# A down tile, late transposes and the prologue's order in an attention and gated-FFN kernel

## The chip, the core and the metric

The kernel runs on one core of a Trainium2 chip. Its time is device microseconds of one launch, as the median of several. The engines of the core work side by side, each on its own queue in the order in which its instructions were written: PE (TensorE) does matmuls, ACT (ScalarE) activations, DVE (VectorE) element-wise work and reductions, POOL (GpSimd) a few small operations, and SP (SyncE) issues nearly all DMAs. They wait for one another through semaphores.

## The reference

The input x has 2048 rows of 512 numbers in bf16. The output is a pre-norm transformer block:

```
h   = x + softmax(q k^T / 4) v @ wo      # q, k, v = layernorm(x) @ wqkv, 32 heads of 16
out = h + (sigmoid(g) * u) @ w_down      # g, u = layernorm(h) @ w_gate, layernorm(h) @ w_up
```

The inner width of the FFN is 1792, which is 14 blocks of 128.

## The kernel before

The prologue loads x, takes the layer norm of the 16 row tiles in pairs (`stats`, `apply`, `trans`), multiplies the first 128 columns of k for all rows (`k_mm`, four heads to a group of 64 columns) and of q for the first 512 rows, and finds a bound on the scores from the norms of q and k, so that the softmax needs no maximum. `k_copy` takes a product of k to SBUF on ACT and sends it to its place by a DMA on SP.

Then come 683 steps. The queries are cut into five chunks, three of 512 rows and two of 256 (`CHUNKS`); in each, 8 groups of four heads go over all keys. A step (`emit_scores`) multiplies the scores of three units of 128 x 512 into the three banks of one of two tiles `pss` (L879), and takes their exponential on ACT (L890). On every fourth step, and some others, ACT takes two banks and DVE computes the third with integer and polynomial operations spread over four steps: L909, L912 and L915, L918, L922. The products with v (`emit_pv`, L961) follow some steps later, mostly on steps whose number is 2 modulo 4, into the one bank `acc`. At the end of each group `emit_norm` copies `acc` (L935), sends the sums through DRAM with DMAs on SP, takes reciprocals (L946) and scales (L942) at fixed later steps.

PSUM has eight banks: six belong to `pss`, one is `acc`, and the last, `pm` (pool `ps_misc`, one buffer), serves everything else while the steps run. This other work is the generator `filler`: the products of v, k and q for later groups, and the FFN of each chunk after its attention is complete. `emit_fill` takes matmuls from it after each step, by a budget (`rate`, per step modulo 4; zero where the step has three PV groups). The generator yields 1 for a matmul, `("at", n)` to go on at the next step that is n modulo 4, `("gap", n)` to leave steps out, `("from", n)` to wait for step n, and `("rate", n)` to set a budget that holds until it is taken back. Deferred work on DVE is put into `later(step, fn)`, which runs ahead of the fill of that step.

The FFN of a chunk is `ffn_tasks`. `ffn_wo_tight`, used for chunks 2 and 3, multiplies a tile of 128 rows with wo in two halves of four matmuls (L598), adds x on DVE (L607), takes statistics (L145, L146, L150, and POOL's power at L152), applies the norm two steps later (L156), and transposes the normalized tile into `pm` (L162) after the next tile's wo. L163 copies the transposed tile to `hnT` on DVE. `ffn_up` takes the 14 blocks in gate and up products (L622), with the tanh (L627) on ACT and the product of both (L635) on DVE, one block to a `pm` tile in chunk 2 and two (of 256 columns each) in chunk 3. `ffn_down` multiplies each tile with w_down in 14 matmuls (L638), and `down_out` forms the output (L643) and stores it (L645).

For the last chunk `wo_early` puts seven of the wo matmuls of the first tile into the steps; the rest is the tail, `ffn_last`, where no attention runs. Its own norm is a chain over DVE, POOL and ACT. While it runs, `spin` keeps PE busy with matmuls into `acc` whose result nobody reads (L253). Then come the last transposes (L791), the copies of h (L806), gate and up blocks, and the down matmuls (L823).

Of the kernel before, what the change touches and what calls it, by code (L numbers as in the profile page):

```python
# [11 lines left out]
FP32 = mybir.dt.float32  # L12
# [7 lines left out]
def kernel(  # L20
# [199 lines left out]
    def k_spread(ku, g, cols, eng):  # L220
        eng.dma_start(out=KT[0:P:2, g, cols], in_=ku[64 * (g % 2):64 * (g % 2) + 64, cols])
# [42 lines left out]
    def prologue(pro):  # L264
# [103 lines left out]
        def k_chunk(n):  # L368
            ps = k_mm(n)
            square(n, ps[:])  # L370
            k_copy(n, ps)
# [47 lines left out]
        apply(4)  # L419
        trans(4)  # L420
        norm_part_of(0)
        k_chunk(1)
        stats(6)
        apply(5)
        trans(5)
        norm_mm_to(acc[:], sqs["q"])
        v0 = v_prod(0, pm_tile())
        v_cast(0, v0)
# [28 lines left out]
        half_copy(0)  # L457
        half_copy(1)
        k_spread(ku, 0, slice(3 * QC, S), nc.sync)
        pn3 = ps_misc.tile([P, 512], FP32, name="pm")  # L460
        norm_half(pn3, 7)
        k_max(pn3[:, 0:QC // 2], km2[:, 2:3])
        v_cast(1, v_prod(1, ps_misc.tile([P, 512], FP32, name="pm")))
        m2 = k_most()
        sqrt_bits(z0[:], m2[:])
        nc.vector.tensor_scalar(out=bnd[0:32, :], in0=y0[0:32, :].bitcast(FP32), scalar1=z0[0:32, :].bitcast(FP32),
# [196 lines left out]
    def ffn_wo_tight(c):  # L663
        turn = None
        for tt, t in enumerate(tiles_of(c)):
            xr = x_load(t)
            yield ("at", 3)
            ps = pm_tile()
            for g in range(NG):
                if g == NG // 2:  # L670
                    yield ("at", 0)
                yield 1
                wo_mm(ps, c, tt, g)
            hn = wo_ln(ps, xr, tt)
            if turn:
                yield ("at", 1)
                yield 1
                hn_transpose(*turn)
            turn = (tt, hn)
        yield ("gap", 1)  # L680
        yield ("at", 1)
        yield 1
        hn_transpose(*turn)

    def ffn_up(c):
        w = CHUNKS[c][1]
        at = cycle((3, 1) if c + 2 < NC else (3, 0, 1))
        for fs in blocks_of(w):
            yield ("at", next(at))
            psg = pm_tile()  # L690
            for i, f in enumerate(fs):
                for k in range(DC):
                    yield w / QC
                    ffn_mm(wg, psg, w, f, i, k)
            sg = gate_act(psg)
            yield ("at", next(at))
            psu = pm_tile()
            for i, f in enumerate(fs):
                for k in range(DC):
                    yield w / QC  # L700
                    ffn_mm(wu, psu, w, f, i, k)
            up_mul(psu, sg, fs, w)

    def ffn_down(c, tight):
        at = 0
        for tt, t in enumerate(tiles_of(c)):
            for f in range(FC):
                if tight:
                    if f % 3 == 0:
                        yield ("at", (3, 0, 1)[at % 3])  # L710
                        at += 1
                elif f % 5 in (0, 3):
                    yield ("at", 0 if f % 5 else 3)
                if f == 0:
                    psd = pm_tile()
                yield 1
                down_mm(psd, f, tt)
            down_out(psd, t, tt)
# [12 lines left out]
    def wo_early(c):  # L731
        early["x"] = [x_load(t) for t in tiles_of(c)]
        early[0] = pm_tile()
        for g in range(NG - 1):
            if g == NG - 2:
                yield ("from", NS - 4)
            yield 1
            wo_mm(early[0], c, 0, g)

    def ffn_last(c):  # L740
        q0, w = CHUNKS[c]
        ts = tiles_of(c)
        n = len(ts)
        sums, rb = pm_tile(), pm_tile()
        pss = [early[0]] + [pm_tile() for _ in range(n - 1)]
        xrs = early["x"]

        def wo(tt, g0, g1):
            for g in range(g0, g1):
                wo_mm(pss[tt], c, tt, g)  # L750

        def add_x(tt):
            nc.tensor.matmul(pss[tt][:], lhsT=ident_bf[:], rhs=xrs[tt][:], start=False, stop=False)

        xs = norm_part(xs_all, w, NG - 1)
        nc.vector.tensor_copy(out=xs, in_=acc[:, 0:w])
        wo(1, 0, 2)
        for q in range(n):
            nc.tensor.matmul(sums[:, 4 * q:4 * q + 4], lhsT=xs[:, q * P:(q + 1) * P],
                             rhs=ident_f[:, DH:P:32], start=True, stop=True)  # L760
        wo(1, 2, 6)
        r16 = small.tile([P, 4 * n], FP32, name="r16")
        nc.vector.reciprocal(out=r16[:], in_=sums[:, 0:4 * n])
        rx = norm_part(rb_all, w, NG - 1).rearrange("p (t j d) -> p t j d", t=n, j=4)
        wide = r16[:].rearrange("p (t j) -> p t j", j=4).unsqueeze(3).to_broadcast([P, n, 4, 32])
        nc.vector.tensor_copy(out=rx[:, 0], in_=wide[:, 0])
        nc.scalar.copy(out=rx[:, 1], in_=wide[:, 1])
        for tt in range(n):
            nc.tensor.matmul(rb[:, tt * P:(tt + 1) * P], lhsT=rx[:, tt].rearrange("p j d -> p (j d)"),
                             rhs=ident_f[:], start=True, stop=True)  # L770
        nc.vector.tensor_tensor(out=OT[c % 2][:, NG - 1, 0:w], in0=xs, in1=rb[:, 0:w], op=ALU.mult)
        ready.add(("o", c, NG - 1))
        wo(1, 6, NG - 1)
        add_x(0)
        add_x(1)
        for tt in range(n):
            wo(tt, NG - 1, NG)
        spin(acc, wo_pad[:, 0, :], 6)
        mv = small.tile([P, n, nc.vector.BN_AGGR_DIM], FP32, name="mvl")
        nmr = small.tile([P, 1], FP32, name="nmr")  # L780
        rss = []
        hns = [pmh["work"].tile([P, D], BF16, name="xn", tag="xn") for _ in range(n)]

        def stats(tt):
            ln_stats(pss[tt][:], mv[:, tt, :])
            rss.append(ln_rstd(mv[:, tt:tt + 1, :], 1))

        def turn(tt, copy):
            pt = pm_tile()[:].bitcast(BF16)[:, 0:4 * P].rearrange("p (b q) -> p b q", b=4)
            for b in range(4):  # L790
                nc.tensor.transpose(out=pt[:, b, :], in_=hns[tt][:, b * P:(b + 1) * P], identity=ident_bf[:])  # L791
            copy(out=hnT[:, :, tt * P:(tt + 1) * P], in_=pt)

        stats(0)
        ln_stats(pss[1][:], mv[:, 1, :])
        nc.vector.tensor_scalar(out=nmr[:], in0=mv[:, 0, 0:1], scalar1=rss[0][:, 0:1], scalar2=-1.0,
                                op0=ALU.mult, op1=ALU.mult)
        nc.scalar.activation(out=hns[0][:], in_=pss[0][:], func=ACT.Identity, scale=rss[0][:, 0:1], bias=nmr[:])
        rss.append(ln_rstd(mv[:, 1:2, :], 1))
        ln_apply(hns[1][:], pss[1][:], mv[:, 1, :], rss[1][:, 0:1])  # L800
        turn(0, nc.scalar.copy)
        spin(acc, wo_pad[:, 0, :], 2)
        turn(1, nc.vector.tensor_copy)
        spin(acc, wo_pad[:, 0, :], 2)
        for tt in range(n):
            nc.vector.tensor_copy(out=h_sb[:, tt, :], in_=pss[tt][:])  # L806
        for fs in blocks_of(w):
            psg = pm_tile()
            for i, f in enumerate(fs):
                for k in range(DC):  # L810
                    ffn_mm(wg, psg, w, f, i, k)
            sg = gate_act(psg)
            psu = pm_tile()
            for i, f in enumerate(fs):
                for k in range(DC):
                    ffn_mm(wu, psu, w, f, i, k)
            up_mul(psu, sg, fs, w)
        for tt, t in enumerate(ts):
            for cols in ((0, D),) if tt < n - 1 else ((0, D // 2), (D // 2, D)):
                cs = slice(*cols)  # L820
                psd = pm_tile()
                for f in range(FC):
                    nc.tensor.matmul(psd[:, cs], lhsT=hT[:, f, tt * P:(tt + 1) * P], rhs=wd[:, f, cs],  # L823
                                     start=(f == 0), stop=(f == FC - 1))
                ob = pmh["work"].tile([P, D], BF16, name="ob", tag="xn")
                nc.vector.scalar_tensor_tensor(out=ob[:, cs], in0=psd[:, cs], scalar=0.5, in1=h_sb[:, tt, cs],
                                               op0=ALU.mult, op1=ALU.add)
                nc.sync.dma_start(out=out_v[:, t, cs], in_=ob[:, cs])

# [145 lines left out]

    def emit_fill(i):
        state["step"] = i
        r = rate(i)
        if not r or state["done"] or i < state["wait"]:
            state["debt"] = 0.0  # L980
            return
# [128 lines left out]
```

## Time and profile before

| what | us |
|---|---|
| median of three runs | 958.11 (957.77 to 960.41) |
| the profiled execution | 958.45 |
| its span | 956.6 |
| first exponential (step 0) starts | 29.82 |
| step 533, first of the late transposes of chunk 2 | 713.85 |
| step 647, first gate block of chunk 3 | 871.19 |
| step 679 | 921.54 |
| end of the last exponential (step 682) | 926.60 |
| first gate block of the tail | 935.30 |
| the stores at the end are issued by | 954.59 |

The step starts are the starts of the L890 rows of the timeline. A row of the timeline has start, length, engine, line, operation, what it writes and reads, and how many instructions were merged into it; in brackets stands how long the engine was idle before it and which instruction ended the wait. A group of rows can merge several steps. The granted clock of TensorE was 1.00 throughout (0.99 in the last 20 us).

### The profile page before, as it was taken

The numbers are of one execution on the slowest core, as the hardware profiler recorded it, in microseconds if no ns is written. First come the engines' busy times: TensorE is split into PE (matmuls) and PEld (weight loads), VectorE is DVE, ScalarE is ACT, GpSimd is POOL, SyncE is SP. The second block draws the span as 40 slices with busy tenths as digits, with TensorE's granted clock in tenths as the row PEclk, the third lists the DMA queues.
The fourth block names the chain that finished last, engine by engine and source line by source line (L and its number), as shares of the span: only waits on it lengthen the run. The fifth ranks groups of instructions, "written<-read, shape, count | busy, mean of one in ns | idle before, by whom it ended". The sixth has DMA issues, their size and how long they took to land.

```text
span 956.6 us, 17273 instructions
## 1 busy us (share of the span) xinstructions
PE 839.0 (88%) x6433; PEld 336.9 (35%) x6433; DVE 783.3 (82%) x1413; ACT 898.2 (94%) x778; POOL 40.0 (4%) x56
## 2 busy tenths in 40 slices
PE   5998888888788999998788999988788999998998
PEld 3322222222222322222222323222355555455656
DVE  7589988888788888899888888898898788777653
ACT  6889999999999999999999999999998999999872
POOL 5600000000000000000000000000000000000000
PEclk9999999999999999999999999999999999999999
DMA  5102350000003000000010000000010000110010
GB/s 161 24 2 56 115 117 16 16 16 14 16 14 103 15 16 17 20 24 23 4 26 27 16 17 16 19 9 27 16 31 23 17 10 15 27 32 16 10 35 12
DMA packets 37645, 28.45 MB, mean 30 GB/s; under 512 B 17788, under 2 KB 32920, under 8 KB 37560
## 3 DMA queue, kind: packets, MB, share of 16 engines
q1 hardware_dynamic: 37416, 27.22, 10.8%
q8 instruction: 50, 0.82, 0.4%
q14 instruction: 35, 0.29, 0.1%
q10 hardware_dynamic: 144, 0.13, 0.0%
HBM read 20.31 MB, written 2.61 MB: 24 GB/s over the span
## 4 chain that ended last, share of the span: by engine, by line
PE 45%; ACT 24%; DVE 22%; issue 6%; DMA 2%; SPq 1%; POOL 0%; ACTq 0%; DVEq 0%
PE pss L879 21%; ACT pt L890 13%; PE acc L961 8%; PE pm L622 7%; ACT stg L890 4%; ACT wd L890 4%; DVE stg L909 2%; PE pm L638 2%; ACT QTu L890 2%; PE pm L598 2%; PE pm L171 2%; DVE y L918 2%; DVE pt L922 2%; DVE reg L912 1%; DVE reg L635 1%
## 5 line engine op out<-in xcount | busy, mean ns | idle before, releaser
L879 PE MATMUL pss<-QB,KT 128*128 128x512 bf16 (+3 forms) x2554 | 476.0, 337 | 80.7 <-ACT pt L890 40.2
L890 ACT ACTIVATE pt<-pss 128x1536 bf16<-128x1536 f32 (+1 forms) x392 | 502.2, 1366 | 14.0 <-PE pss L879 9.5
L879 PEld LDWEIGHTS <-KT 64*128 64x128 bf16 (+1 forms) x2554 | 179.3, 95 | 340.5 <-issue 232.8
L890 ACT ACTIVATE stg<-pss 128x1536 bf16<-128x1536 f32 (+1 forms) x140 | 183.4, 1361 | 5.0 <-PE pss L879 3.8
L909 DVE TENSOR_SCALAR stg<-pss 128x512 int32<-128x512 f32 x123 | 84.8, 690 | 68.1 <-PE pss L879 59.9
L961 PE MATMUL acc<-pt,Vaug 128*17 128x512 bf16 (+1 forms) x1471 | 112.5, 338 | 2.3 <-DVE pt L922 1.1
L890 ACT ACTIVATE wd<-pss 128x1536 bf16<-128x1536 f32 (+1 forms) x80 | 103.9, 1391 | 1.9 <-PE pss L879 1.4
L890 ACT ACTIVATE QTu<-pss 128x1024 bf16<-128x1024 f32 (+1 forms) x71 | 95.9, 1350 | 1.7 <-PE pss L879 1.3
L915 DVE SCALAR_TENSOR_TENSOR y<-reg 128x512 f32<-128x512 f32 x123 | 85.2, 692 | 4.2
L918 DVE SCALAR_TENSOR_TENSOR y<-y,reg 128x512 f32<-128x512 f32 x123 | 84.3, 685 | 1.1
L961 PEld LDWEIGHTS <-Vaug 128*17 128x17 bf16 x2560 | 49.2, 89 | 94.7 <-issue 80.3
L622 PE MATMUL pm<-reg,reg 128*128 128x512 bf16 (+1 forms) x280 | 57.9, 337 | 7.9 <-DVE reg L635 7.6
L622 PE MATMUL pm<-reg,wu 128*128 128x512 bf16 (+1 forms) x280 | 58.1, 338 | 1.4 <-ACT sg L627 1.1
L638 PE MATMUL pm<-wd,reg 128*128 128x512 bf16 x196 | 55.6, 382 | 1.9 <-DVE ob L643 1.9
L912 DVE TENSOR_SCALAR reg<-stg 128x512 int32<-128x512 int32 x123 | 52.0, 422 | 1.8
L961 PE MATMUL acc<-stg,Vaug 128*17 128x256 bf16 (+1 forms) x564 | 50.6, 326 | 0.3 <-DVE stg L922 0.2
L635 DVE SCALAR_TENSOR_TENSOR reg<-sg,pm 128x512 bf16<-128x512 f32 x56 | 38.2, 683 | 14.2 <-PE pm L622 13.8
L922 DVE SCALAR_TENSOR_TENSOR pt<-y,stg 128x512 bf16<-128x512 f32 x70 | 48.0, 686 | 2.0
L152 POOL TENSOR_TENSOR rs<-ve,pw_neg 128x1 f32<-128x1 f32 x16 | 11.8, 735 | 877.1 <-DVE ve L150 870.5
L627 ACT ACTIVATE sg<-pm 128x512 f32<-128x512 f32 x56 | 36.5, 651 | 10.4 <-PE pm L622 9.9
L909 DVE TENSOR_SCALAR wd<-pss 128x512 int32<-128x512 f32 x45 | 31.0, 689 | 17.9 <-PE pss L879 16.5
L171 PE MATMUL pm<-reg 128*128 128x512 bf16 x124 | 38.3, 398 | 1.8 <-DVE stg L526 0.7
(151 smaller groups left out, 715.8 us busy)
## 6 DMA issues: line engine op xcount, KB each, us to landing
rb_all<-rd SPq DMA_DIRECT2D x96, 64.0 KB
xr<-in_A_x_dram SPq DMA_DIRECT2D x16, 128.0 KB
out_dram<-ob SPq DMA_DIRECT2D x15, 128.0 KB
rb_all<-rd SPq DMA_DIRECT2D x60, 32.0 KB
reg<-in_A_x_dram SPq DMA_DIRECT2D x7, 256.0 KB
KT<-stg SPq DMA_DIRECT2D x7, 256.0 KB
reg<-in_B_w_gate_dram SPq DMA_DIRECT2D x4, 448.0 KB
wu<-in_B_w_up_dram SPq DMA_DIRECT2D x4, 448.0 KB
```

Of the source, the lines that this page charges most:

```text
L171: nc.tensor.matmul(ps[:], lhsT=wqkv_sb[:, c, w0:w0 + P], rhs=xnT[:, c, n * QC:(n + 1) * QC], start=(c == 0), stop=(c == DC - 1))
L622: nc.tensor.matmul(ps[:, i * w:(i + 1) * w], lhsT=wt[:, c, f * P:(f + 1) * P], rhs=hnT[:, c, 0:w], start=(c == 0), stop=(c == DC - 1))
L635: nc.vector.scalar_tensor_tensor(out=out, in0=a, scalar=1.0, in1=b, op0=ALU.add, op1=ALU.mult)
L638: nc.tensor.matmul(ps[:], lhsT=hT[:, f, tt * P:(tt + 1) * P], rhs=wd[:, f, :], start=(f == 0), stop=(f == FC - 1))
L879: nc.tensor.matmul(pss[:, ui, h * w:(h + 1) * w], lhsT=KT[rows, g, kt * P:(kt + 1) * P], rhs=QB[n_qg % 2][rows, j, 0:w], start=True, stop= ...
L890: ex = nc.scalar.activation(out=pt[:, 0:na, :], in_=pss[:, 0:na, :], func=ACT.Exp, scale=DH ** -0.5 / QS)
L909: return nc.vector.tensor_scalar(out=e_bits, in0=src, scalar1=ONE_BITS, scalar2=0.0, op0=ALU.add, op1=ALU.max)
L912: nc.vector.tensor_scalar(out=e_man, in0=e_bits, scalar1=0x7FFFFF, scalar2=-0x40800000, op0=ALU.bitwise_and, op1=ALU.bitwise_or)
L915: nc.vector.scalar_tensor_tensor(out=e_pol, in0=m, scalar=PA, in1=m, op0=ALU.add, op1=ALU.mult)
L918: nc.vector.scalar_tensor_tensor(out=e_pol, in0=e_pol, scalar=PB, in1=e_man.bitcast(FP32), op0=ALU.add, op1=ALU.mult)
L922: nc.vector.scalar_tensor_tensor(out=dst, in0=e_pol, scalar=PC, in1=e_bits.bitcast(FP32), op0=ALU.add, op1=ALU.mult)
L961: nc.tensor.matmul(acc[32 * j:32 * j + VW, 0:w], lhsT=Vaug[:, kt, 4 * g + j, :], rhs=p[:, h * w:(h + 1) * w], start=(kt == 0), stop=(kt == ...
```

## The change

There are four parts.

In the prologue, the ACT copy of the second 512 columns of k (`k_copy(1)`) goes behind the copy of the transposed tiles 10 and 11 (`trans(5)`). The product of v for tile 1 goes into `acc` instead of `pm`, with two of its four matmuls ahead of the last norm product (`norm_half(pn3, 7)`) and two behind it.

The transposes in `ffn_wo_tight` ask for a step that is 2 modulo 4 instead of 1. These are four tiles in chunk 2 (steps 533, 537, 541, 545 become 534, 538, 542, 546) and two in chunk 3 (641, 645 become 642, 646). `emit_fill` lets fill run on such a step while a rate is set.

The gate and up blocks of chunk 3 are put on five steps out of eight instead of six out of eight.

The down matmuls of the last tile of chunk 3 leave the steps. They stand in the tail in the place of the six `spin` matmuls ahead of the norm's transposes; their output is formed after the copies of h, which now take two other rows of `h_sb`. The early wo matmuls of the last chunk follow directly, and the seventh of them comes after the last PV.

```diff
@@ prologue
-        k_chunk(1)
+        ps1 = k_mm(1)
+        square(1, ps1[:])
         stats(6)
         apply(5)
         trans(5)
+        k_copy(1, ps1)
...
+        for c in range(2):
+            v_mm(acc, 1, c)
         pn3 = ps_misc.tile([P, 512], FP32, name="pm")
         norm_half(pn3, 7)
         k_max(pn3[:, 0:QC // 2], km2[:, 2:3])
-        v_cast(1, v_prod(1, ps_misc.tile([P, 512], FP32, name="pm")))
+        for c in range(2, DC):
+            v_mm(acc, 1, c)
+        v_cast(1, acc)
@@ ffn_wo_tight, twice
-                yield ("at", 1)
+                yield ("at", 2)
                 yield 1
                 hn_transpose(*turn)
@@ ffn_up
-        at = cycle((3, 1) if c + 2 < NC else (3, 0, 1))
+        at = cycle((3, 1) if c + 2 < NC else (3, 1, 3, 0, 1))
@@ ffn_down
-        for tt, t in enumerate(tiles_of(c)):
+        for tt, t in enumerate(tiles_of(c)[:None if c < NC - 2 else -1]):
@@ wo_early
-                yield ("from", NS - 4)
+                for _ in range(3):
+                    yield ("from", NS + LAG)
@@ ffn_last
-        spin(acc, wo_pad[:, 0, :], 6)
+        psd = pm_tile()
+        for f in range(FC):
+            down_mm(psd, f, len(tiles_of(c - 1)) - 1)
...
         for tt in range(n):
-            nc.vector.tensor_copy(out=h_sb[:, tt, :], in_=pss[tt][:])
+            nc.vector.tensor_copy(out=h_sb[:, n + tt, :], in_=pss[tt][:])
+        down_out(psd, tiles_of(c - 1)[-1], len(tiles_of(c - 1)) - 1)
...
-                nc.vector.scalar_tensor_tensor(out=ob[:, cs], in0=psd[:, cs], scalar=0.5, in1=h_sb[:, tt, cs],
+                nc.vector.scalar_tensor_tensor(out=ob[:, cs], in0=psd[:, cs], scalar=0.5, in1=h_sb[:, n + tt, cs],
@@ emit_fill
-        r = rate(i)
+        r = rate(i) or i % CYC == 2 and state["rate"]
```

## The prediction

> **What bounds the kernel now.** I read the page first (busy shares, then the chain that ended last), then busy time by stretches, then the timeline of the three places that the change touches.
>
> ```profile
> span 956.6 us, 17273 instructions
> PE 839.0 (88%) x6433; PEld 336.9 (35%) x6433; DVE 783.3 (82%) x1413; ACT 898.2 (94%) x778; POOL 40.0 (4%) x56
> PE 45%; ACT 24%; DVE 22%; issue 6%; DMA 2%; SPq 1%; POOL 0%; ACTq 0%; DVEq 0%
> ```
>
> ACT is busiest, yet the chain runs mostly over PE: an average over stages. Where ACT sets the pace, exponentials (L890) start 1.33 to 1.35 us apart, 0.90 on every fourth step, whose third bank DVE takes: 4.91 for a cycle of four steps. "Step n" is exponential n, counted from 0; step starts are those of the L890 rows in the timeline.
>
> ```profile
> 871.00:905.00 34.00, 30.55 (x340) 21.57 (x339) 21.93 (x40) 29.71 (x28) 0.00 (x0) 1.00 0.05 12
> 905.00:927.00 22.00, 21.06 (x249) 11.72 (x247) 12.50 (x23) 20.64 (x17) 0.00 (x0) 1.00 0.13 37
> ```
>
> The columns after the length are PE, weight loads, DVE, ACT and POOL busy. These two stretches are the FFN of chunk 3 (the last but one): PE is nearly full. Steps 647 to 679 take 50.35 us (871.19 to 921.54) where ACT's pace would need about 40.5. Here a PE instruction removed is time removed.
>
> The late transposes stand in a stage where DVE is the tight one:
>
> ```profile
> 721.98 0.69 DVE L915 SCALAR_TENSOR_TENSOR y<-reg 128x512 f32<-128x512 f32 x1
> 722.59 0.42 DVE L163 COPY reg<-pm 128x512 bf16<-128x512 bf16 x1
> 722.92 0.41 DVE L935 COPY xs_all<-acc 128x256 f32<-128x256 f32 x1
> 723.06 1.02 PE L598 MATMUL pm<-wo_pad,OT 128*128 128x512 bf16 x4 [1.01 <-DVE reg L163]
> 723.25 0.68 DVE L918 SCALAR_TENSOR_TENSOR y<-y,reg 128x512 f32<-128x512 f32 x1
> 723.85 0.54 DVE L156 TENSOR_SCALAR xn<-reg,mv,rs 128x512 bf16<-128x512 f32 x1
> ...
> 725.49 1.02 ACT L890 ACTIVATE pt<-pss 128x1024 bf16<-128x1024 f32 x1 [1.42 <-PE pss L879]
> ```
>
> The one bank `pm` holds the transposed tile until L163 has copied it; the next tile's wo matmuls (L598) wait 1.01 us for that, the next scores stand behind them in PE's queue, and ACT idles 1.42.
>
> At the start, from 20 to 30 us:
>
> ```profile
> 20.33 0.62 ACT L361 CAST stg<-pm 128x512 bf16<-128x512 f32 x1
> 20.80 1.07 ACT L341 COPY reg<-pm 128x1024 bf16<-128x1024 bf16 x1
> ...
> 26.59 0.28 PE L387 MATMUL pm<-sq,ones_blk 128*128 128x256 bf16 x1 [0.58 <-DVE km L179]
> 27.38 1.02 PE L166 MATMUL pm<-reg 128*128 128x512 bf16 x4 [0.52 <-DVE km L179]
> 28.24 0.81 PE L866 MATMUL pss<-QB,KT 128*128 128x512 bf16 x3
> 28.89 0.81 PE L869 MATMUL pss<-bnd,ident_bf 128*128 128x512 bf16 x3
> 29.82 1.45 ACT L890 ACTIVATE pt<-pss 128x1536 bf16<-128x1536 f32 x1 [0.79 <-PE pss L869]
> ```
>
> PE waits twice for DVE's maxima (0.58, 0.52), and from 27.38 works without a pause until the first steps.
>
> **Part 1, prologue: 1.0 us less.** On ACT the copy of xnT (L341) goes ahead of L361, so it starts at 20.33 instead of 20.80. The k_mm(2) matmuls at 21.92 waited for it (0.39), and square, norm, transposes and maxima follow from them: 0.45 earlier. L361's output is sent by SP, which is busy with the eight QB DMAs until 23.64; L361 ends at 21.8 then, so the DMA is covered by 1.8 us. Second, two of the four v matmuls of tile 1 (marginal 0.26 each, 0.52) fit the 0.58 wait ahead of L387, and the other two follow it without a wait, as they now write `acc`, last read at 22.5. The first scores then end ahead of `bnd`, ready at 28.22, so L869 starts at 28.25 instead of 28.89: 0.6 more. Both ends: 1.1 if neither QB row nor DMA stops step 2, 0.4 if only the first gain stays because the two `bnd` DMAs, issued from 28.25, stop the second. I take 1.0: step 2 started at 31.79 with no wait on them. PE is continuous from here to about 40 us, so the gain stays.
>
> **Part 2, late transposes: 3.0 us more.** The changed rate lets fill run in the step with PV; by the order of the instructions only these transposes use it. The four transposes of each late tile (marginal 0.22 on PE) move behind the PV matmuls of the next step. PE no longer waits for L607 (0.47, 0.24, 0.24), but ACT lost only 0.1 by that. On DVE, L163 moves behind L918 and L156 (0.60 and 0.45 from start to start) and in two places behind L935 (0.33). So the wo matmuls of chunk 2's third tile start 1.05 later, and the scores and the exponential behind them too; L909 of that step must wait for these scores, so DVE is late by the same 1.05 and catches nothing up. For the fourth tile the copy stands another 0.33 + 0.60 + 0.45 = 1.38 further back: 2.43 in all. The copy of the fourth tile itself (step 545, now 546) stands behind L935 and L918 and ends at 735.06 instead of 733.52, so that the first gate block waits 0.98, from 734.12; ACT had 0.37 in hand there (its tanh starts 0.64 after that block's end at 735.16), so 0.6 stays. The third tile's copy, and the first of chunk 3, have no user within two steps: 0, their cover being a step without fill, and 1.05 or 1.38 if a user came there. The last one of chunk 3 keeps its place on DVE and puts 0.22 of transposes ahead of PV: 0.2, kept in part 3. Sum 1.05 + 1.38 + 0.6 = 3.0. Ends: nothing, if DVE had these two instructions done ahead; 5.8, if all five delayed copies cost their delay (1.05, 1.38, 1.05, 0.98, 1.38). I am near the middle as each of the three counted has a waiting matmul in the timeline.
>
> The Trainium skill ("Perfetto Trace Analysis", section Matmuls) says that independent matmul groups should rotate through PSUM banks, so that one group's evacuation overlaps the next group's matmuls. This kernel has one bank left for all fill work, so by that sentence every later evacuation costs its delay; the sum of part 2 would be 5.8 rather than 3.0. The 1.01 us wait above agrees; that step 543, which has no fill, started on ACT's pace (1.33) speaks against it for the third tile.
>
> **Part 3, FFN of chunk 3: 3.1 us less.** Before, by cycles from step 647: 7.50, 6.53, 6.94, 6.56 (three blocks each), 6.34 (two blocks at steps 663, 664), then 5.49, 5.68, 5.31 with down matmuls: 50.35. After, the 14 blocks go two, three, two, three, two, two to a cycle, and one tile's 14 down matmuls follow. A cycle with two blocks is in the trace: in chunk 2, fourteen cycles from 734.47 to 811.44 mean 5.50, 5.54 without two extra split steps; 5.37 the shortest, 5.98 the longest of the regular ones. So 3 x 5.54 = 16.6; three blocks 6.94 (gate, up, gate) and 6.56 (up, gate, up); steps 667 and 668 like 663 and 664, 6.34; five down groups, 5.49 and 5.06 (5.68 without its third group): 47.0. That is 3.3 less, minus 0.2 from part 2. Ends: 1.0 less, if two-block cycles take 5.98 and three-block ones 7.2; 4.2, at 5.37 and 6.53. The early wo matmuls stand at steps 679 to 681, where ACT sets the pace (1.33 each): 0. SP issues the last output and the two x loads after the norm's DMAs instead of ahead of them: 0.4 on the norm's way to its product at 925.91, ahead of the last wo matmul at 926.86, which waits for PV anyway: 0.
>
> **Part 4, tail: 0.0 us.**
>
> ```profile
> 930.69 1.46 PE L253 MATMUL acc<-wo_pad,ident_bf 128*128 128x512 bf16 x6
> 933.66 0.40 PE L791 MATMUL pm<-ident_bf,xn 128*128 128x128 bf16 x4 [1.51 <-ACT xn L798]
> ```
>
> The 14 down matmuls replace the six L253: 14 x 0.216 (L823 issues at that rate) = 3.02 in a slot of 933.66 - 930.69 = 2.97. The second transposes wait for DVE until 934.38, which takes up the 0.05. The output's arithmetic on DVE (L643, 0.69) fits between the h copies, done at 936.44, and the first L635 at 937.33. If that cover goes, +0.7; a gain is excluded as nothing leaves the path.
>
> **The sum.** -1.0 + 3.0 - 3.1 + 0.0 = -1.1 on the profiled execution's 958.45 (span 956.6 and 1.85 around it): 957.3. That execution stands 0.34 above the median of 958.11, so I forecast 957.0. A difference of 0.3% (2.9 us) is about what a measurement of this kernel can tell from no change; the forecast lies within it.
>
> **Rivals.**
> A, faster: the moved copies cost nothing, since the matmuls that wait for them would wait for something else. For it: ACT idled 0.41 and 1.42 there already. Against it: L915 and L163 follow each other with DVE never idle. It decides if L163 ends before the next tile's scores have issued. 957.0 - 3.0 = 954.0; down to 952.9 with part 3 at its best.
> B, slower: one bank serves wo, transposes and blocks, and each of the six moved transposes costs the largest ACT idle that stands behind such a copy, 1.42: 8.5 instead of 3.0, so 962.5. It ends slower than before from 0.7 each on, and slower by 0.3% from 1.15 each. For it: the 1.01 wait. Against: three of six have no user close behind. The skill's sentence on rotating banks is this rival's rule.
> C, the spreading gains nothing: DVE stops at L946 for the sums' DMA (1.26 idle ahead of 874.78, in the 7.50 cycle) in more cycles as steps get shorter, and the blocks wait for L635 behind it. 957.0 + 3.1 = 960.1. Against: chunk 2's cycles run at 5.50 with the same norms.
>
> **How the numbers follow.** Forecast 0.46, A 0.32, B 0.16, C 0.06. The forecast's own range is 955.2 to 959.8 (part 2 between 1.2 and 5.8, the others at their values). Of the forecast 0.04 falls under 955.2 and counts as faster, and of C 0.02 over 961.0 as slower: faster 0.36, same 0.46, slower 0.18. The range from 953.3 to 961.4 holds the forecast, C, all of A but its lowest 0.05 and leaves most of B out.
>
> **What would show it.** Prologue: first exponential at 28.8. Transposes: L163 after L156, PE waiting about 1.5 us at the fourth tile's wo; ACT idle near 2 us instead of 0.41 before step 536, and over 2 before 540; step 548 about 2 us later than in before. FFN: steps 647 to 679 in 47 us. Tail: L791 within 0.1 of the end of the down matmuls. Wrong if these waits do not appear, or if cycles with two 256-wide blocks exceed 6 us.

## The result, and the profile after

The changed kernel takes 963.67 us (median of 9, 961.68 to 967.16), the kernel before beside it 959.2 (median of 9, 957.77 to 961.05): a ratio of 1.0049, interval 1.0033 to 1.0065. It is slower, by more than the 0.3% that can be told from no change, where 957.0 was forecast. The profiled execution of after took 961.68 us (span 959.9), the shortest of the nine.

The page of after, its busy shares and its chain:

```profile
span 959.9 us, 17266 instructions
PE 838.5 (87%) x6427; PEld 335.7 (35%) x6427; DVE 783.7 (82%) x1413; ACT 897.1 (93%) x778; POOL 40.0 (4%) x56
PE 44%; DVE 24%; ACT 22%; issue 6%; DMA 2%; SPq 1%; POOL 0%; ACTq 0%; DVEq 0%
```

The busy times are those of before to about 1 us; a reader of the page alone would not see what happened. The starts of the exponentials show it. Where a stage begins and ends at a numbered step, its length can be set beside the other kernel's:

| stage (by step) | before | after | difference | forecast |
|---|---|---|---|---|
| start to step 0 | 29.82 | 28.60 | -1.22 | -1.0 |
| 0 to 535 | 686.85 | 687.32 | +0.47 | 0 |
| 535 to 548, late transposes | 19.60 | 28.09 | +8.49 | +3.0 |
| 548 to 647 | 134.92 | 134.62 | -0.30 | 0 |
| 647 to 679, FFN of chunk 3 | 50.35 | 46.33 | -4.02 | -3.1 |
| 679 to the end | 35.09 | 34.92 | -0.17 | 0.0 |

The differences sum to +3.25, which is the span's. One stage of 20 us holds the loss. Its timeline in after (start, length, engine, line, operation, count, and in brackets the idle time ahead of it with what ended that):

```profile
717.32 1.02 PE L604 MATMUL pm<-wo_pad,OT 128*128 128x512 bf16 x4 [1.77 <-DVE reg L163]
717.36 2.47 SPq L238 DMA_DIRECT2D QB<-QTu  x4
719.10 1.02 ACT L900 ACTIVATE stg<-pss 128x1024 bf16<-128x1024 f32 x1 [1.72 <-PE pss L889]
719.88 1.25 SPq L248 DMA_DIRECT2D QB<-bnd  x2
721.18 0.39 SPq L609 DMA_DIRECT2D xr<-in_A_x_dram  x1
723.37 0.69 DVE L613 TENSOR_TENSOR reg<-pm,xr 128x512 f32<-128x512 f32 x1 [3.58 <-DMA xr<-in_A_x_dram]
724.11 0.38 PE L162 MATMUL pm<-ident_bf,xn 128*128 128x128 bf16 x4 [2.62 <-DVE reg L613]
725.13 1.45 ACT L900 ACTIVATE pt<-pss 128x1536 bf16<-128x1536 f32 x1 [1.84 <-PE pss L889]
727.49 0.54 DVE L156 TENSOR_SCALAR xn<-reg,mv,rs 128x512 bf16<-128x512 f32 x1
727.94 0.42 DVE L163 COPY reg<-pm 128x512 bf16<-128x512 bf16 x1
728.41 1.86 PE L604 MATMUL pm<-wo_pad,OT 128*128 128x512 bf16 x4 [3.38 <-DVE reg L163]
732.49 1.02 ACT L900 ACTIVATE pt<-pss 128x1024 bf16<-128x1024 f32 x1 [5.91 <-PE pss L889]
```

The first wait is the forecast's: the wo matmuls (L604, L598 before) wait 1.77 us for the copy L163, which stands behind L156 (as at 727.49 and 727.94), and ACT idles 1.72. Then come two things that the forecast does not have. The x load of the third late tile, which SP issued at 716.83 before, ahead of the six QB DMAs, is issued at 721.18, behind them; the addition that needs it waits 3.58, and through the bank `pm` TensorE waits 2.62. SP's queue in before, at the same place:

```profile
716.83 0.42 SPq L603 DMA_DIRECT2D xr<-in_A_x_dram  x1
717.35 2.47 SPq L238 DMA_DIRECT2D QB<-QTu  x4
719.88 1.26 SPq L248 DMA_DIRECT2D QB<-bnd  x2
```

And the four wo matmuls at 728.41 take 1.86 us instead of 1.02. The windows of that stretch (length, then PE, weight loads, DVE, ACT and POOL busy with their counts, then the granted clock) say why:

```profile
722.00:724.00 2.00, 0.00 (x0) 0.00 (x0) 0.63 (x1) 1.30 (x1) 0.00 (x0) 1.00 0.21 66
724.00:726.00 2.00, 0.93 (x10) 0.60 (x10) 1.86 (x7) 0.87 (x1) 0.63 (x1) 0.80 0.00 0
726.00:728.00 2.00, 0.00 (x0) 0.00 (x0) 2.00 (x5) 0.58 (x1) 0.00 (x0) 0.50 0.00 1
728.00:730.00 2.00, 1.59 (x4) 0.41 (x3) 0.96 (x3) 0.00 (x0) 0.00 (x0) 0.50 0.01 2
730.00:732.00 2.00, 2.00 (x22) 0.99 (x22) 0.00 (x0) 0.00 (x0) 0.00 (x0) 0.50 0.23 67
```

TensorE is busy for 0.93 us of the 6.4 from 722.00 to 728.41, and its granted clock is 0.50 from 725.18 for 6.83 us, just when the work that everything waits for comes. The loss by step, after less before: 1.32 into step 536, 1.95 into 539, 4.48 into 540, 0.27 into 547 and 0.47 into 548.

The prologue, the FFN stage (the same columns as the windows above) and the tail in after:

```profile
26.30 0.42 DVE L179 TENSOR_REDUCE km<-pm 128x1 f32<-128x256 f32 x1 [0.38 <-PE pm L387]
27.68 0.81 PE L879 MATMUL pss<-bnd,ident_bf 128*128 128x512 bf16 x3 [0.28 <-DVE nks L475]
28.60 4.13 ACT L900 ACTIVATE pt<-pss 128x1536 bf16<-128x1536 f32 x3 [1.28 <-PE pss L879]
```

```profile
878.60:912.40 33.80, 31.83 (x367) 22.57 (x366) 23.40 (x42) 31.38 (x30) 0.00 (x0) 1.00 0.06 13
912.40:930.30 17.90, 16.60 (x207) 9.38 (x205) 10.35 (x20) 17.62 (x14) 0.00 (x0) 1.00 0.15 40
```

```profile
933.95 3.19 PE L644 MATMUL pm<-wd,reg 128*128 128x512 bf16 x14
936.98 0.39 PE L800 MATMUL pm<-ident_bf,xn 128*128 128x128 bf16 x4
```

The first scores end with L879 at 27.68, 1.21 us ahead of L869 in before, released by the end of the arithmetic on the bound (nks); the FFN stage is still one in which PE is nearly full, only shorter; and L800 (L791 before) starts within 0.2 of the end of the 14 down matmuls.

### The profile page after: what moved, and what is told of

Read it like the earlier page. It is cut to its first block, busy times and chain, and to the rows that moved or that the text cites. A ratio compares the mean times of both kernels' runs of the same rounds, so it can differ in the third digit from the quotient of the medians.

```text
span 959.9 us, 17266 instructions
## 1 busy us (share of the span) xinstructions
PE 838.5 (87%) x6427; PEld 335.7 (35%) x6427; DVE 783.7 (82%) x1413; ACT 897.1 (93%) x778; POOL 40.0 (4%) x56
## 4 chain that ended last, share of the span: by engine, by line
PE 44%; DVE 24%; ACT 22%; issue 6%; DMA 2%; SPq 1%; POOL 0%; ACTq 0%; DVEq 0%
PE pss L889 21%; ACT pt L900 13%; PE acc L971 8%; PE pm L628 7%; ACT stg L900 4%; ACT wd L900 4%; DVE stg L919 2%; PE pm L644 2%; ACT QTu L900 2%; DVE y L928 2%; PE pm L604 2%; DVE pt L932 2%; DVE reg L922 2%; DVE y L925 1%; DVE st L145 1%
## 5 line engine op out<-in xcount | busy, mean ns | idle before, releaser
L604 PE MATMUL pm<-wo_pad,OT 128*128 128x512 bf16 x128 | 34.4, 388 | 5.2 <-DVE reg L163 5.1
(152 smaller groups left out, 717.5 us busy)
```

The costliest lines, as they stand in the source:

```text
L604: nc.tensor.matmul(ps[:], lhsT=OT[c % 2][:, g, tt * P:(tt + 1) * P], rhs=wo_pad[:, g, :], start=(g == 0), stop=(g == NG - 1))
```

## The experiments

In the first four expectations, theory 1 is that the x load which went along with the transposes makes up what the sum lacked, and theory 2 that it does not (the copies cost their 3.0 or, in e3, everything). "Stage" below is the length of steps 535 to 548: 19.60 us before, 28.09 after.

**e1: the changed kernel with the late transposes a step back.**

```diff
-                yield ("at", 2)
+                yield ("at", 1)
 ...
-        yield ("at", 2)
+        yield ("at", 1)
```

> The changed kernel with the late transposes back on the steps that are 1 modulo 4; its prologue, the spreading of chunk 3's blocks and the moved down tile stay. The trace of the changed kernel loses 8.4 us between steps 533 and 548. Theory 1 (the third tile's x load stands on SP behind six QB DMAs, DVE waits for it, PE idles and its clock is halved): all of this goes, 963.7 - 8.4 = 955.3, which is 0.4% under before. Theory 2 (the recorded one: only the later copy L163 on DVE costs, 3.0): 960.7.

Measured 955.1 us (953.93 to 955.48), ratio 0.9962 (0.9951 to 0.9974); the stage takes 19.61. The loss is in these two lines: 963.67 - 955.1 = 8.6 us. Without them the change is faster than before.

**e2: the kernel before with the transposes a step on and the rate that lets them run there, nothing else.**

```diff
-                yield ("at", 1)
+                yield ("at", 2)
 ...
-        yield ("at", 1)
+        yield ("at", 2)
 ...
-        r = rate(i)
+        r = rate(i) or i % CYC == 2 and state["rate"]
```

> The kernel before with the transposes moved alone (and the rate that lets fill run there). Theory 1: 959.2 + 8.4 = 967.6, DVE waiting about 3.6 us for the x load at step 537 and the granted clock halved for some 7 us. Theory 2: 959.2 + 3.0 = 962.2, with no wait on the x load.

Measured 969.94 us (968.88 to 970.68), ratio 1.0118 (1.0105 to 1.0132), the stage 28.99. The part alone costs 11.6, more than within the whole change; the granted clock of its profiled execution is 0.50 for 10.24 us from 726.5 and for 3.41 us at three other places.

**e3: the changed kernel with each x load issued where it was, ahead of the moved transposes.**

```diff
-        turn = None
-        for tt, t in enumerate(tiles_of(c)):
-            xr = x_load(t)
+        turn, ts = None, tiles_of(c)
+        nxt = x_load(ts[0])
+        for tt, t in enumerate(ts):
+            xr = nxt
 ...
             if turn:
+                yield ("at", 1)
+                if tt + 1 < len(ts):
+                    nxt = x_load(ts[tt + 1])
                 yield ("at", 2)
                 yield 1
                 hn_transpose(*turn)
+            elif tt + 1 < len(ts):
+                nxt = x_load(ts[tt + 1])
```

> The changed kernel with the next tile's x load issued before the transposes, where SP had it before; the order on PE, ACT and DVE is the changed kernel's. Theory 1: DVE's wait for x goes, PE's longest idle time falls under 2 us and the clock stays at 1.00; what is left of the transposes is the later copy, about 3.0, so 955.3 + 3.0 = 958.3. If the copy costs nothing either: 955.3. Theory 2: the x load is hidden anyway, so no change, 963.7.

Measured 961.82 us (960.6 to 963.66), ratio 1.0037 (1.0023 to 1.0051), the stage 27.25. Theory 1 fails here: with the loads on time the moved transposes still cost 961.82 - 955.1 = 6.7 us, not 3.0. Its timeline:

```profile
717.26 0.42 SPq L609 DMA_DIRECT2D xr<-in_A_x_dram  x1
717.64 0.59 PE L604 MATMUL pm<-wo_pad,OT 128*128 128x512 bf16 x1 [1.77 <-DVE reg L163]
720.88 1.02 ACT L906 ACTIVATE stg<-pss 128x1024 bf16<-128x1024 f32 x1 [3.19 <-PE pss L895]
726.92 1.11 PE L604 MATMUL pm<-wo_pad,OT 128*128 128x512 bf16 x4 [2.40 <-DVE reg L163]
730.47 1.02 ACT L906 ACTIVATE pt<-pss 128x1024 bf16<-128x1024 f32 x1 [3.93 <-PE pss L895]
```

TensorE's first wait is the same 1.77 as in after, yet ACT idles 3.19 behind it instead of 1.72: here the clock record falls to 0.50 at 717.5, at 727.7 and at 738.0, for 3.41 us each. Step 536 loses 2.78 at half clock and lost 1.32 in after at full clock. The forecast's 1.05 is near what the copy costs at full clock; what it lacked is that the clock may fall.

**e4: the kernel before with the x loads of the third and fourth late tile moved behind the QB DMAs, and the rate that lets the generator go on in that step.**

```diff
         for tt, t in enumerate(tiles_of(c)):
+            if tt > 1:
+                yield ("at", 2)
+                yield 0
             xr = x_load(t)
 ...
-        r = rate(i)
+        r = rate(i) or i % CYC == 2 and state["rate"]
```

> The kernel before with nothing moved but the third late tile's x load, which SP now issues behind the six QB DMAs of the next step; transposes and copies stay. Theory 1: the load is issued at about 721.2 instead of 716.8 and lands near 723.3, so L607 starts 4.0 later and the transposes, scores and exponentials with it: 959.2 + 4.0 = 963.2, and up to 1.7 more if PE's idle time of about 4 us halves the clock. Theory 2: 959.2, unchanged.

Measured 964.91 us (962.23 to 967.93), ratio 1.0067 (1.0047 to 1.0086), the stage 24.70.

```profile
721.30 0.39 SPq L603 DMA_DIRECT2D xr<-in_A_x_dram  x1
723.47 0.69 DVE L607 TENSOR_TENSOR reg<-pm,xr 128x512 f32<-128x512 f32 x1 [3.60 <-DMA xr<-in_A_x_dram]
726.12 1.45 ACT L893 ACTIVATE QTu<-pss 128x1536 bf16<-128x1536 f32 x1 [4.08 <-PE pss L882]
```

The load issued behind the six DMAs, with no transposes moved, costs 964.91 - 958.33 = 6.6 us: both consequences of the move are dear by themselves. Together they cost 8.6 and not 13.3; their waits lie in the same cycles.

**e5 and e6: the other parts alone.** e5 is the kernel before with the FFN and tail edits, e6 with the prologue edits.

```diff
-        at = cycle((3, 1) if c + 2 < NC else (3, 0, 1))
+        at = cycle((3, 1) if c + 2 < NC else (3, 1, 3, 0, 1))
 ...
-        for tt, t in enumerate(tiles_of(c)):
+        for tt, t in enumerate(tiles_of(c)[:None if c < NC - 2 else -1]):
 ...
-        spin(acc, wo_pad[:, 0, :], 6)
+        psd = pm_tile()
+        for f in range(FC):
+            down_mm(psd, f, len(tiles_of(c - 1)) - 1)
 ...
```

```diff
-        k_chunk(1)
+        ps1 = k_mm(1)
+        square(1, ps1[:])
         stats(6)
         apply(5)
         trans(5)
+        k_copy(1, ps1)
 ...
+        for c in range(2):
+            v_mm(acc, 1, c)
 ...
-        v_cast(1, v_prod(1, ps_misc.tile([P, 512], FP32, name="pm")))
+        for c in range(2, DC):
+            v_mm(acc, 1, c)
+        v_cast(1, acc)
```

> The kernel before with the FFN and tail parts of the change alone (gate and up blocks of chunk 3 spread over more steps, its last down tile and the copies of h in the tail); transposes and prologue as before. Theory 1 (the parts add up: steps 647 to 679 shrink by 4.0 us as they did in the changed kernel, the tail by 0.15): 958.3 - 4.1 = 954.2 us, steps 647 to 679 in about 46.3. Theory 2 (the 4.0 us of that stage were there only because the transposes came late and shifted what meets what): steps 647 to 679 stay above 48 us and the time above 956.

> The kernel before with the prologue part alone (second K chunk's copy later, second V product split around the max). Theory 1 (the first exponential starts 1.2 us earlier and about 0.6 of that lasts, as in the changed kernel): 958.3 - 0.6 = 957.7 us, with 957.1 if all but 0.0 of it lasts. Theory 2 (what is gained ahead of step 0 is given back in the first steps): 958.3.

e5 measured 955.09 us (954.7 to 956.03), ratio 0.9965 (0.9952 to 0.9978), steps 647 to 679 in 46.17: the FFN and tail part is all of the gain. e6 measured 958.68 us (957.36 to 960.89), ratio 1.0001 (0.9991 to 1.0011): the prologue part is worth nothing, though its first exponential starts at 28.60. e5, which has the old prologue, starts its first at 29.24, so 0.64 of the 1.22 us that the two profiled executions of before and after show is the part's, and the rest differs from execution to execution.

**e7 and e9: the waits made shorter and longer.** e7 is e3 with the late tiles' normalisation (L156) a step later, so that the copy goes ahead of it; e9 is e1 with the late copies done three times.

```diff
-    def wo_ln(ps, xr, tt):
+    def wo_ln(ps, xr, tt, lag=2):
 ...
-        later(state["step"] + 2, lambda: ln_apply(hn[:], h_sb[:, tt, :], mv[:, 0, :], rs[:, 0:1]))
+        later(state["step"] + lag, lambda: ln_apply(hn[:], h_sb[:, tt, :], mv[:, 0, :], rs[:, 0:1]))
 ...
-            hn = wo_ln(ps, xr, tt)
+            hn = wo_ln(ps, xr, tt, 3 if tt + 1 < len(ts) else 2)
```

```diff
+        def thrice(out, in_):
+            for _ in range(3):
+                nc.vector.tensor_copy(out=out, in_=in_)
 ...
-                hn_transpose(*turn)
+                hn_transpose(*turn, thrice)
 ...
```

> The changed kernel with each x load ahead of the late transposes (as in e3), and the normalisation of the late tiles (0.54 us on VectorE) one step later, so that the copy of the transposes no longer stands behind it. TensorE's waits of 1.77 and 2.40 us for that copy should fall to about 1.2 and 1.9. Theory 1 (the granted clock falls because TensorE waits that long, and each half-clock stretch of 3.41 us costs about 1.3 us): with the clock at 1.00 through steps 533 to 548 the time is 961.8 - 3 x 0.54 - 3 x 1.3 = 956.3 us; if a wait of 1.9 is still long enough for one stretch, 957.6. Theory 2 (the waits cost their own length, the clock record is a by-product): 961.8 - 1.6 = 960.2 us.

> The changed kernel with the transposes a step back (as e1, 955.1 us) and the copy of each late tile's transposes done three times, so that TensorE's single transposing bank comes free 0.84 us later at each of them. Theory 2 (a wait costs its own length): at most 3 x 0.84 = 2.5 us, 957.6 us, granted clock 1.00 around steps 533 to 548. Theory 1 (waits of some 1.2 to 1.9 us here make the granted clock fall for one to three stretches of 3.41 us, 1.3 us each): 958.9 to 961.5 us, with half-clock stretches between 715 and 740 us.

e7 measured 959.63 us (957.15 to 964.46), ratio 1.0011 (0.9997 to 1.0025), the stage 23.65: between the two theories. e9 measured 961.46 us (959.77 to 966.0), ratio 1.0034 (1.0022 to 1.0046), the stage 22.39, 2.78 more than e1's: the 2.5 of theory 2, although the time itself is where theory 1 put it. The wo matmuls of the fourth late tile, in e7 and then in e9 (L672 is the repeated copy):

```profile
724.03 1.02 PE L604 MATMUL pm<-wo_pad,OT 128*128 128x512 bf16 x4 [1.94 <-DVE reg L163]
727.29 1.02 ACT L906 ACTIVATE pt<-pss 128x1024 bf16<-128x1024 f32 x1 [3.19 <-PE pss L895]
```

```profile
727.88 1.04 PE L604 MATMUL pm<-wo_pad,OT 128*128 128x512 bf16 x4 [1.93 <-DVE reg L672]
730.32 1.02 ACT L904 ACTIVATE pt<-pss 128x1024 bf16<-128x1024 f32 x1 [2.35 <-PE pss L893]
```

The same wait, 1.94 and 1.93. In e7 the clock falls to 0.50 at 725.3 for 3.41 us, and ACT idles 3.19; in e9 it stays at 1.00 through the stage, and ACT idles 2.35. So a wait of this length does not decide whether the clock falls. In e9 it fell elsewhere, for 6.83 us at 80.8 and 3.41 at 248.1 (e1: 3.41 at 81.7); of the 6.6 us between the spans of e9 and e1, 2.46 lie ahead of step 535, 2.78 in the stage and 1.4 behind it, where chunk 3's late tiles copy three times too.

**e10 and e11: the copy's cover put back.** Both do all eight wo matmuls of a late tile in one step, so that two steps' scores stand between the transposes and the next user of the bank; e10 is otherwise e3, e11 otherwise e1.

```diff
-            yield ("at", 3)
+            yield ("at", 0)
             ps = pm_tile()
             for g in range(NG):
-                if g == NG // 2:
-                    yield ("at", 0)
                 yield 1
```

> The changed kernel with x loads ahead of the late transposes (as e3, 961.8 us) and all eight output-projection matmuls of a late tile in one step, a step later than their first half stood, so that two steps' score matmuls stand between a tile's transposes and the matmuls that need the bank back. To be read against e11, which has the same projection order with the transposes a step back. Theory 1 (what the moved transposes cost beside the x load is TensorE's wait for their copy, and with it the clock): with the wait covered by the 1.3 us of score matmuls, this run is within 1 us of e11, instead of 6.7 us above as e3 is of e1. Theory 2 (the transposes cost by their place in step 2 itself, among the P.V matmuls, whatever follows them): 4 us or more above e11.

> The changed kernel with the late transposes a step back (as e1, 955.1 us) and the eight output-projection matmuls of a late tile in one step instead of four and four. Eight in a row are 2.04 us of TensorE where four were 1.02; if the two score buffers cover the extra 1.02 the time is 955.1, and the wait of 1.01 us for the copy that e1 still shows goes with it (954.5); if they cover none of it, up to six late tiles x 1.02 = 961.2. Both theories expect 955 to 958: it is the base for e10.

e10 measured 971.32 us (969.71 to 973.21), ratio 1.013 (1.0113 to 1.0147), and e11 969.33 (967.56 to 970.89), ratio 1.0112 (1.0091 to 1.0132). The base missed its expectation by 11 us and more: against e1's profiled execution e11 loses 3.4 us ahead of step 535, 7.7 between 548 and 647 and 2.7 between 647 and 679; why eight matmuls in a row cost so much there I have not followed further. The comparison holds all the same: e10 is 2.0 above e11, not 6.7 (nor within 1; the ranges of the four runs each overlap), and the stage takes 19.40 in e10 and 19.04 in e11, at full clock in both, with the transposes at step 2 in the one and at step 1 in the other. In e10 TensorE waits 0.20 us for the copy:

```profile
727.07 0.42 DVE L163 COPY reg<-pm 128x512 bf16<-128x512 bf16 x1
727.54 1.89 PE L604 MATMUL pm<-wo_pad,OT 128*128 128x512 bf16 x8 [0.20 <-DVE reg L163]
```

So in this stage it is not their place in step 2 that costs, but that the matmuls which need the bank follow too soon.

**e12 and e13: where the prologue's gain goes.** GpSimd's memsets of K^T, in the first steps, cut into four; e12 is otherwise e6, e13 otherwise e1.

```diff
-                nc.gpsimd.memset(KT[:, 2 * b + n // 2, :], 1.0)
+                for q in range(4):
+                    nc.gpsimd.memset(KT[:, 2 * b + n // 2, q * QC:(q + 1) * QC], 1.0)
```

> The kernel before with the prologue part alone (as e6, 958.7 us) and GpSimd's memsets of K^T, 128x2048 each, cut into four of 128x512. In e6 the VectorE operation that takes 0.42 us elsewhere takes 1.93 us at 41.91 and ends 0.28 us after GpSimd's memsets do (43.56); the V casts behind it are late, and of the 0.64 us that the first exponential gained on the executions with the old prologue 0.5 is gone by step 16. Theory 1 (the memset holds VectorE back): the operation falls to under 0.9 us, the stretch from step 0 to 535 from 687.44 to about 686.9, the time to 958.2. Theory 2 (the order of the V products itself gives the gain back): the operation, 687.4 and 958.7 stay.

> The changed kernel with the late transposes a step back (as e1, 955.1 us) and the same memsets cut into four: a version that may beat both kernels by the most. Theory 1: 955.1 - 0.5 = 954.6 us. Theory 2: 955.1 us.

e12 measured 959.48 us (957.53 to 961.97), ratio 1.0009 (0.9998 to 1.0019), e13 954.84 (954.49 to 955.85), ratio 0.9963 (0.9951 to 0.9975). The edit went the wrong way and showed the cause by that. The end of GpSimd's memsets and the VectorE operation, in e5 (old prologue), in e6 (new) and in e12 (new, memsets cut):

```profile
40.04 3.54 POOL L529 MEMSET KT<- 128x2048 bf16 x2
42.55 1.31 DVE L916 TENSOR_SCALAR reg<-wd 128x512 int32<-128x512 int32 x1
```

```profile
40.02 3.54 POOL L535 MEMSET KT<- 128x2048 bf16 x2
41.91 1.93 DVE L918 TENSOR_SCALAR reg<-wd 128x512 int32<-128x512 int32 x1
```

```profile
40.50 3.78 POOL L536 MEMSET KT<- 128x512 bf16 x8
41.92 2.65 DVE L919 TENSOR_SCALAR reg<-wd 128x512 int32<-128x512 int32 x1
```

The memsets end at 43.58, 43.56 and 44.28, the operation at 43.86, 43.84 and 44.57: 0.28 or 0.29 behind them each time, whenever it began. Elsewhere it takes 0.42. The new prologue brings VectorE to it 0.64 us earlier and it ends no earlier.

**e14, e15 and e16: the memsets' chain made shorter.** One of the two 128x2048 memsets of the padded weights, which stand in the same chain, goes to VectorE in the prologue; e14 is otherwise e6, e15 the kernel before, e16 e1.

```diff
+        nc.vector.memset(wo_pad[:, 0:4, :].bitcast(FP32), 0.0)
         nc.vector.memset(Vaug[:, :, :, DH:DH + 1], 1.0)
 ...
-        for g4 in (0, 4):
-            later(60 + g4, lambda g4=g4: nc.gpsimd.memset(wo_pad[:, g4:g4 + 4, :], 0.0))
+        later(64, lambda: nc.gpsimd.memset(wo_pad[:, 4:8, :], 0.0))
```

> The kernel before with the prologue part alone (as e6, 958.7 us), and one of the two 128x2048 memsets of the projection's padded weights taken out of GpSimd's chain: VectorE does it at 2.4 us, where it has 1.67 us of nothing to do. GpSimd's chain ends 1.77 us earlier, at 41.8. Theory 1 (that chain holds back a VectorE operation at step 12 and with it everything after): the operation takes about 0.4 instead of 1.93 us, and the run is 0.6 us below e15, with e15 itself 0.3 to 0.9 below before. Theory 2 (the new order of the V products gives its gain back by itself): within 0.2 us of e15.

> The kernel before with the same memset moved to VectorE at 2.4 us. Theory 1: the VectorE operation that took 1.31 us at 43.13 takes 0.42, all steps from 13 on come up to 0.9 us earlier: 957.6 to 958.2 us. Theory 2 (the operation's length is hidden behind the V products): 958.6 us, as before.

> The changed kernel with the late transposes a step back (as e1, 955.1 us) and the same memset moved to VectorE. Theory 1: 955.1 - 0.6 to 1.5 = 953.6 to 954.5 us. Theory 2: 955.1 us.

e14 measured 959.26 us (957.97 to 962.59), ratio 1.0006 (0.9997 to 1.0015), e15 958.32 (957.94 to 959.67), ratio 1.0 (0.9992 to 1.0009), e16 955.56 (953.79 to 958.11), ratio 0.9965 (0.9952 to 0.9979). In e15 and then in e14 the operation comes after the memsets and takes its normal time:

```profile
39.38 3.54 POOL L530 MEMSET KT<- 128x2048 bf16 x2
43.63 0.42 DVE L913 TENSOR_SCALAR reg<-wd 128x512 int32<-128x512 int32 x1
```

```profile
39.37 3.54 POOL L536 MEMSET KT<- 128x2048 bf16 x2
43.01 0.44 DVE L919 TENSOR_SCALAR reg<-wd 128x512 int32<-128x512 int32 x1
```

And the prologue's lead now lasts: e14's step 0 is 0.62 ahead of e15's, its step 16 still 0.63, where e6's lead over e5 was 0.64 at step 0 and 0.07 at step 16. That is theory 1 as far as the trace can show. The times do not follow it: the memset on VectorE starts the first step 1.1 us later (30.32 in e15 against 29.24 in e5), which eats what the shorter chain gives, and e14 lies 0.9 above e15 and not 0.6 below. In e14's profiled execution the clock is at half for 10.24 us, at 81.6 and 248.8. At equal granted clock the two differ by less: 958.02 us (2 runs of e14) against 958.09 (6 of e15) at 1.000, and 959.26 (7) against 959.44 (5) at 0.998. So most of the 0.6 us does not reach the end even then; where it goes behind step 16 is not shown.

The best versions are e1, e5 and e13, 954.8 to 955.1 us, which these runs do not tell apart: the FFN and tail part is what all three share.

## Why the prediction was wrong

**Part 2, "3.0 us more"**, is the step that failed; measured 8.6 (after less e1) and +8.49 in the stage. By the terms of its sum, the third tile's 1.05 came out at 1.32 (step 536) and the first gate block's 0.6 at 0.74 (steps 547 and 548), but the fourth tile's 1.38 at 6.43 (steps 539 and 540). Two things were missing, and in after both fall on that term.

First, an instruction that went along. The forecast named the four transposes and their copy. But `ffn_wo_tight` issues the next tile's x load as soon as the transposes are out, so moving them moved the load to a later place on SP, behind the six QB DMAs of the same step. Its price was in the trace of before: the six take 2.47 + 1.26 us of SP's queue from 717.35 to 721.14, and the load, issued at 716.83 then, would follow at 721.2, as it did. The forecast looked at the last tiles' loads only. e4 shows the price: 6.6 us alone.

Second, the clock. The profile of before has 1.00 in this stage, and the sum took each wait at its own length. At full clock that comes near: the term of 1.05 measured 1.32 in after; e9's added waits of at most 2.5 us cost 2.78. But in after, e2, e3, e4 and e7 the clock fell in this stage, in or just behind TensorE's waits, and the matmuls for which all else waits ran at half speed. The time of a run follows its mean granted clock, in steps of about one half-clock stretch of 3.41 us (1.7 of 960 us of full-speed work, 0.0018). For before, over its runs beside e1, e5, e10, e12 and e14, and for after:

| granted clock | before: median us (runs) | after: median us (runs) |
|---|---|---|
| 1.000 | 957.47 (28) | none |
| 0.998 | 958.83 (39) | none |
| 0.996 | 960.12 (21) | 962.05 (3) |
| 0.995 | none | 963.64 (2) |
| 0.993 | none | 964.75 (3) |
| 0.989 | none | 967.16 (1) |

A stretch costs some 1.3 us, in before (957.47 to 960.12 for two) as in after (962.05 to 967.16 for four). The median run of after has three stretches, that of e1 one (0.998): of the 8.6 us about 2 x 1.3 = 2.6 are the clock, and about 6 are waits at full clock, where 3.0 was forecast. The same sum leaves 4.1 of e3's 6.7 us to the moved copies and 4.0 of e4's 6.6 to the late load (three stretches in the median run of both); the two overlap in after. e2's runs have four or six stretches (0.993 and 0.989), so about 5 of its 11.6 us are the clock. These divisions are estimates from the table, not measured apart.

The Trainium skill ("TensorE: Matmul & The Clock Gate", section What's actually happening) has the clock go to half after about one idle window of 3.4 us, the windows running freely. The length of the stretches agrees (3.41, 6.83 and 10.24 us), and so does the free running: in all 17 traces the clock changes only at whole multiples of 3.413 us from the first entry of its record, which comes 14.8 to 17.8 us into the span. That a whole idle window is needed does not: in e3 it fell after a wait of 1.77, with TensorE busy before and behind.

**Part 1, "1.0 us less ... so the gain stays"**, failed too: e6 gives 0.0, interval -0.9 to +1.1. Half of the -1.22 at step 0 was the execution's; of the other 0.64, 0.58 is left at step 12 and 0.07 at step 13, where VectorE waits for GpSimd's memsets (e12) whenever it comes there. I followed PE, ACT and SP through the prologue but not GpSimd, whose row on the page says 4% busy. The Trainium skill ("SBUF — State Buffer", section Who interferes with whom) has a VectorE operation in a two-port mode and a GpSimd one exclude each other, the later one blocked until the first instruction ends. The blocking agrees, though no run shows the mode that the operation ran in; but with memsets of about 0.47 us (3.78 for eight) the operation was held for 2.65 - 0.42 = 2.2 us, to the end of the whole chain and not of one instruction.

**Part 3, "3.1 us less"**, was right in mechanism and too small: 3.7 by e5's time (958.83 to 955.09), 4.0 in the stage. By cycles from step 647, after takes 5.39, 7.16, 5.93, 6.03, 5.39, 6.39, 4.98 and 5.06. The three two-block cycles (5.39, 5.93, 5.39) sum to 16.7 where I took 16.6. What was too long in the forecast is the three-block cycles, 7.16 and 6.03 (13.2 where I took 13.5), and above all the down groups, 4.98 and 5.06 (10.0 where I took 10.55).

**Part 4, "0.0"**, was right: steps 679 to the end 34.92 against 35.09.

**The rivals.** B, the one that ended slower, gave 962.5, and the time came out 1.2 above it, but that is chance: its mechanism (all six copies at 1.42 each) is not what happened: the loss is in chunk 2's stage alone (chunk 3's late tiles, steps 640 to 647, take 9.40 us against 9.19), and it is due to a load and the clock as well as to the copies. That the copies cost nothing (A) fell with e3, that the spreading gains nothing (C) with e5. Of what was named as a sign, L163 behind L156, ACT's idle of nearly 2 us ahead of step 536, the FFN stage and the tail came as told; the wait at the fourth tile's wo was 3.38 instead of 1.5, and step 548 came 7.74 later instead of 2.

## What to carry to other kernels

When a step of a generator or a planner is moved, list every instruction that it issues until its next pause, on every queue, and set each beside its new neighbours there; the dear one here was a DMA that the diff doesn't mention. A wait that leaves TensorE idle for some 2 us can cost its length and then half-speed matmuls behind it, for 3.41 us or a multiple; a sum of waits is a lower end where the stage has no slack. And before a gain at the start is kept to the end, look for a chain on another engine, however idle that is on the page, that everything meets later.

## What had not been expected of the hardware

The granted clock halves for 3.41 us or a multiple in some executions of every kernel here, before too, and at places where TensorE's longest wait in 8 us was 0.75 (at 81.7 in e1). The same wait of 1.93 to 1.94 us left it at 1.00 in e9 and was followed by 0.50 in e7. The traces say more when they are divided at the multiples of 3.413 us at which the clock changes. The last four stretches of each trace left out, the 17 traces hold 4585 such stretches at full clock. TensorE is busy for 0.61 of the stretch or less in 82 of them, and all 29 falls to half clock come right behind one of these 82. The seven emptiest (busy for 0.43 or less) were all followed by a fall, among them the one from 721.77 in after (0.27) and the one from 721.85 in e7 (0.43); the emptiest of before has 0.58. So a fall goes with how much of one fixed stretch TensorE is idle, and the same wait can lie within one stretch or across two. That is not the whole rule: the stretch from 725.97 in e9 has 0.44 and was not followed by a fall, and 53 of the 82 were not either. What decides there is open.

A VectorE integer operation of 0.42 us took up to 2.65 beside a chain of GpSimd memsets and ended 0.28 or 0.29 us after the chain, in three kernels with two different chains (e5 and e6; e12).
